# Keys of the second batch projected 64 tokens at a time, one halved step instead of two, and another order of work

## The chip, the cores and the metric

The kernel runs on one core of a Trainium2 chip. The time is that of the device, in microseconds (us), for one launch; the measure is the median of several executions. The core has five engines that run side by side, each taking its own instructions in the order in which they were written: TensorE (PE in the profile; its weight loads are listed apart as PEld), VectorE (DVE), ScalarE (ACT), GpSimd (POOL), and SyncE (SP), which here issues all transfers between memory and the chip. They wait for each other through semaphores.

## The reference

Linear attention over four batches of 1088 tokens, whose features are outer products of two small projections, followed by a gated two-layer network:

```python
def phi(x):
    a = np.einsum('rd,bhsd->bhsr', S1, x)
    b = np.einsum('rd,bhsd->bhsr', S2, x)
    return np.einsum('bhsi,bhsj->bhsij', a, b).reshape(*x.shape[:-1], r * r)
q_p, k_p = (phi(q), phi(k))                     # r = 8, 64 features
kv = np.einsum('bhsf,bhsd->bhfd', k_p, v)
z = np.sum(k_p, axis=2)
num = np.einsum('bhsf,bhfd->bhsd', q_p, kv)
den = np.einsum('bhsf,bhf->bhs', q_p, z)[..., None] + 1e-06
x = (num / den), reshaped to 4352 tokens x 128
h = x @ w_in                                    # 128 x 2048
g = h * np.clip(h + 3.0, 0.0, 6.0) / 6.0
out = g @ w_out                                 # 2048 x 128
```

## The kernel before

The whole schedule is written out by hand: `ORDER` is a string of some 1,070 names, and `Plan.run` emits one operation after the other in that order. As each engine takes its own instructions in program order, `ORDER` fixes for each engine what comes behind what. A name may carry a choice after a colon: `:V` puts the operation on VectorE instead of its first engine, `:a`, `:h`, `:o` choose the bank of PSUM. `warm` is a matmul of ones that nobody reads (L284).

The inputs arrive as loads (`ld_...`, L324), all issued by SyncE in the order of the string: keys k0 to k7 (two pieces for each batch), values v0 to v7, queries q0 to q8, and the weights in five blocks of w_in (wi0 to wi4) and four of w_out (wo0 to wo3). A load waits until its buffer is free: the weights' raw words have 4 buffers, the keys 3, the values 3. Weights come as 64-bit words that hold float32; `scale`, `rest` (ScalarE or VectorE), `shift` (VectorE), `word` (GpSimd or VectorE), `high` (ScalarE) and `low` (GpSimd or VectorE) turn a block into a high and a low part, since each large product is done as three matmuls: high x high, low x high, high x low.

For each batch the keys are projected (`mm_k`, L377), copied out (`cp_k`), their outer products made (`outer_k`), and summed against the values on TensorE, tile by tile of 128 tokens (`kvt_b_i`, L407 and L410); `twice_b`, `fold_b` and `keep_b` bring the sum into the form that the queries use. `mm_k` projects a tile of 128 tokens in pieces of KEY_COLS[b] tokens; s_all, 64 columns, is what streams. Batch 0 takes pieces of 64, batches 1 to 3 pieces of 32.

The 4352 tokens form nine chunks. Chunk 0 goes the near way (`tr`, `trcp`, `nd`, `norm`, `xt`), with `halves` (L438) bringing the first batch's sum to it; the others go the far way (`proj`, `cp`, `prod`, `invert`, `divide`, `outer`, `turn`, `move`, `xmm`), where `move` is a set of transfers within the chip. `xhi` and `xlo` split x into two parts. Then come eight steps for each chunk, two blocks of 128 hidden units each: `h` and `l` (L632, L633, L636) form h in a bank of type h, of which there are two; `relu` (ScalarE), `gate` (VectorE), `ghi` (ScalarE or VectorE) and `glo` (GpSimd or VectorE) form the gated value and its two parts; `o` and `p` (L669) add up the output, `out` brings it out of PSUM and `store` writes it. A step that is halved (chunk below HALVED, step below FIRST) makes its h in two halves of 256 tokens, so that it can begin when half of x is there; its parts are named `h_c_step_block_half`.

```python
halved = c < HALVED and fp < FIRST
for r, u in product(range(2 if halved else 1), range(2)):
    i, k = (r * n // 2, (r + 1) * n // 2) if halved else (0, n)
```

Of the kernel before, what the change touches and what calls it, by code (L numbers as in the profile page):

```python
# [107 lines left out]
fold_1 cp_k5 outer_k5_0:V h_0_1_1_0 turn_1_0 high_wi3 ghi_0_3 h_0_1_0_0 l_0_1_0_0 outer_1_1 h_0_1_0_1 turn_1_1 l_0_1_1_0 ld_q3 h_0_2_1 l_0_2_1
scale_wi4 outer_k5_4:V h_0_2_0 l_0_2_0 shift_wi4 keep_1 low_wi3 h_0_1_1_1 l_0_1_1_1 outer_k5_2:V relu_0_2 ld_q2 l_0_1_0_1 relu_0_1 o_0_3 gate_0_2
ld_wo0 rest_wo0 rest_wi4 scale_wo0 mm_k4 gate_0_1 move_1 proj_23:o:a cp_2_1 cp_2_0 shift_wo0 h_0_5_1 l_0_5_1 ld_k6 ld_v4 h_0_5_0 ghi_0_2 glo_0_2:V  # L110
cp_3_1 h_0_4_1 cp_3_0 glo_0_3 l_0_5_0 word_wi4 l_0_4_1 high_wi4 low_wi4 cp_k4 h_0_4_0 l_0_4_0 relu_0_5 gate_0_5 p_0_3 relu_0_4 gate_0_4 o_0_2 p_0_2
ghi_0_1 xmm_1:o:a xhi_1_0 xlo_1_0 xhi_1_1 xlo_1_1 word_wo0 h_0_6_1 l_0_6_1 high_wo0 h_0_6_0 l_0_6_0 outer_k4_0:V h_1_1_0 ghi_0_0 outer_k4_2:V ld_v5
ld_q4 l_1_1_0 h_1_1_1 relu_0_6 l_1_1_1 prod_3 invert_3 glo_0_1 relu_1_1 gate_0_6 kvt_2_0 kvt_2_1 kvt_2_2 kvt_2_3 kvt_2_4 kvt_2_5 kvt_2_6 mm_k6 cp_k6
kvt_2_7 low_wo0 kvt_2_8 twice_2 h_1_2_0 l_1_2_0 ghi_0_4 glo_0_0:V glo_0_4 gate_1_1 h_1_2_1 l_1_2_1 relu_1_2 p_0_1 ghi_1_1 prod_2 p_0_0 h_1_3_0
outer_k6_0:V l_1_3_0 h_1_3_1 ld_v6 ld_q7 l_1_3_1 relu_1_3 ld_k7 divide_3 outer_3_1 gate_1_2 outer_3_0 glo_1_1:V o_0_1 gate_1_3 ld_wo3 ld_v7 h_0_7_1
invert_2 ghi_1_2 h_0_7_0 l_0_7_0 ld_wo2 scale_wo2 l_0_7_1 relu_0_7 o_0_0 outer_k6_2:V h_1_0_1 h_1_0_0 l_1_0_0 gate_0_7 turn_3_1 rest_wo3 l_1_0_1
fold_2 out_0_3 mm_k7 kvt_3_0 kvt_3_1 h_1_7_1 glo_1_2 turn_3_0 divide_2 outer_2_0 outer_2_1 h_1_7_0 l_1_7_0 l_1_7_1 o_1_2 ghi_1_3 glo_1_3:V relu_1_0
p_1_2 gate_1_0 relu_1_7 p_1_3 h_1_5_0 l_1_5_0 ld_q5 gate_1_7 ghi_1_0 glo_1_0 turn_2_1 turn_2_0 cp_k7:V h_1_5_1 scale_wo3 outer_k7_2:V l_1_5_1 keep_2
o_1_1 shift_wo3 h_1_6_1 shift_wo2 word_wo3:V rest_wo2 l_1_6_1 h_1_6_0 l_1_6_0 word_wo2 p_1_1 o_1_0 ghi_0_7 outer_k7_4 p_1_0 relu_1_5 gate_1_5 o_1_3
h_1_4_0 l_1_4_0 ghi_0_5 outer_k7_0:V glo_0_7:V h_1_4_1 l_1_4_1 high_wo3:V high_wo2 out_1_3 move_3 low_wo2:V ghi_0_6 glo_0_6 proj_45:a:o cp_4_1  # L120
relu_1_6 cp_5_1 kvt_3_2 kvt_3_3 kvt_3_4 kvt_3_5 kvt_3_6 cp_4_0 kvt_3_7 kvt_3_8 twice_3 cp_5_0 gate_1_6 move_2 xmm_23:o:a xhi_3_1 fold_3 o_0_4 relu_1_4
xhi_3_0:V h_3_1_1 h_3_1_0 xlo_3_1 xlo_3_0 l_3_1_0 low_wo3 glo_0_5:V p_0_6 xhi_2_0 xlo_2_0 l_3_1_1 gate_1_4 xhi_2_1 ghi_1_6 relu_3_1 glo_1_6 gate_3_1
p_0_4 o_0_6 ghi_1_4 xlo_2_1 glo_1_4:V h_3_3_0 h_3_3_1 l_3_3_1 prod_4 l_3_3_0 relu_3_3 p_0_5 ld_q6 invert_4 divide_4 h_3_0_0 l_3_0_0 o_0_7 p_0_7
outer_4_0 gate_3_3 ghi_3_1 glo_3_1:V o_1_6 h_3_0_1 l_3_0_1 h_2_0_1 l_2_0_1 h_2_0_0 p_1_6 relu_3_0 l_2_0_0 relu_2_0 ghi_1_7:V keep_3 gate_3_0 o_0_5
ghi_1_5 h_2_1_0 l_2_1_0 glo_1_7 prod_5 gate_2_0 h_2_1_1 l_2_1_1 p_1_7 glo_1_5 out_0_7 h_3_2_0 l_3_2_0 h_3_2_1 l_3_2_1 p_1_4 relu_2_1 gate_2_1 relu_3_2
o_1_5 invert_5 ghi_3_3:V h_3_5_0 l_3_5_0 o_1_4 glo_3_3 h_3_5_1 gate_3_2 l_3_5_1 o_1_7 ghi_2_1 glo_2_1:V divide_5 relu_3_5 gate_3_5 h_2_3_0 l_2_3_0
h_2_3_1 l_2_3_1 relu_2_3 p_1_5 p_3_1 gate_2_3 o_3_1 outer_4_1 ghi_3_2 glo_3_2:V h_3_6_1 h_3_6_0 l_3_6_1 ghi_3_0 glo_3_0 l_3_6_0 relu_3_6 outer_5_1
# [638 lines left out]
```

## Time and profile before

| | us |
|---|---|
| median of 3 runs | 225.82 |
| lowest and highest | 225.63, 226.63 |
| the profiled execution, its own time | 226.31 |
| its span, first to last instruction | 224.4 |
| TensorE busy in the span | 218.4 (97%) |
| VectorE busy | 182.2 (81%) |
| ScalarE busy | 147.7 (66%) |
| GpSimd busy | 144.2 (64%) |

The span is the stretch between the first and the last instruction that the profiler saw; the time of the execution is 1.9 us longer. Durations below come from this one execution. A matmul's end is modelled, so the distance from one start to the next tells more than the duration of one.

### The profile page before, as it was taken

The page shows a single profiled execution, that of the slowest core. Times are in us where ns is not written, and L with a number is a line of the kernel's source. Part 1 is how long each engine was busy: PE and PEld are TensorE (multiplying, and loading weights), DVE is VectorE, ACT ScalarE, POOL GpSimd, SP SyncE. Part 2 cuts the span into 40 slices and gives each one's busy share as a digit, 9 for nine tenths or more (in the row PEclk, how much of TensorE's full clock was granted, in tenths as well). Part 3 has the DMA queues.
Part 4 walks back from the last instruction along what each step waited for, and adds up shares of the span by engine and source line. Part 5 has one row for each costly group of instructions (what it writes and reads, how often), then busy time and mean ns, then how long its engine had stood idle before and what let it go on. Part 6 is the DMA issues. An engine that isn't in the chain of part 4 may idle for free.

```text
span 224.4 us, 4722 instructions
## 1 busy us (share of the span) xinstructions
PE 218.4 (97%) x1885; PEld 175.5 (78%) x1885; DVE 182.2 (81%) x244; ACT 147.7 (66%) x201; POOL 144.2 (64%) x103
## 2 busy tenths in 40 slices
...
DMA packets 9429, 17.76 MB, mean 79 GB/s; under 512 B 1728, under 2 KB 2368, under 8 KB 9408
## 3 DMA queue, kind: packets, MB, share of 16 engines
...
## 4 chain that ended last, share of the span: by engine, by line
PE 93%; DMA 2%; SPq 1%; ACT 1%; issue 1%
PE o L669 42%; PE h L632 14%; PE h L633 14%; PE h L636 14%; DMA raw<-weights_dram 2%; PE o L407 2%; PE a L377 2%; PE a L546 1%; PE a L551 1%; SPq L324 1%; PE o L551 1%; ACT w L339 1%; PE o L546 0%; PE h L513 0%; PE o L501 0%
## 5 line engine op out<-in xcount | busy, mean ns | idle before, releaser
L652 POOL TENSOR_TENSOR gl<-g,gh 128x1024 fp32r<-128x1024 f32 (+1 forms) x39 | 92.1, 2364 | 60.9 <-ACT gh L254 34.2
L646 DVE SCALAR_TENSOR_TENSOR g<-g,h 128x1024 f32<-128x1024 f32 (+1 forms) x72 | 82.6, 1154 | 20.1 <-ACT g L643 19.7
L643 ACT ACTIVATE g<-h 128x1024 f32<-128x1024 f32 (+1 forms) x72 | 70.1, 979 | 36.6 <-PE h L636 23.9
L254 ACT CAST gh<-g 128x1024 fp32r<-128x1024 f32 (+1 forms) x53 | 53.2, 1011 | 19.3 <-PE o L669 16.7
L632 PE MATMUL h<-xh,wi_hi 128*128 128x512 f32 (+1 forms) x148 | 55.8, 378 | 0.0
L633 PE MATMUL h<-xh,wi_lo 128*128 128x512 f32 (+1 forms) x148 | 55.0, 373 | 0.0
L669 PE MATMUL o<-gh,wo_hi 128*128 128x512 f32 (+1 forms) x144 | 54.3, 381 | 0.0
L669 PE MATMUL o<-gh,wo_lo 128*128 128x512 f32 (+1 forms) x144 | 54.0, 378 | 0.0
L636 PE MATMUL h<-xh,wi_hi 128*128 128x512 f32 (+1 forms) x148 | 52.7, 372 | 0.0
L652 DVE TENSOR_TENSOR gl<-g,gh 128x1024 fp32r<-128x1024 f32 (+1 forms) x33 | 40.8, 1238 | 4.6 <-ACT gh L254 3.6
L669 PE MATMUL o<-gl,wo_hi 128*128 128x512 f32 (+1 forms) x144 | 40.9, 379 | 0.0
L632 PEld LDWEIGHTS h<-xh,wi_hi 128*128 128x128 f32 x148 | 27.8, 188 | 7.1 <-DVE g L646 0.6
L633 PEld LDWEIGHTS h<-xh,wi_lo 128*128 128x128 f32 x148 | 27.9, 188 | 4.7
L636 PEld LDWEIGHTS h<-xh,wi_hi 128*128 128x128 f32 x148 | 27.6, 188 | 5.0
L669 PEld LDWEIGHTS o<-gh,wo_hi 128*128 128x128 f32 x144 | 27.1, 188 | 5.5 <-issue 0.4
L669 PEld LDWEIGHTS o<-gh,wo_lo 128*128 128x128 f32 x144 | 27.1, 188 | 4.9
L669 PEld LDWEIGHTS o<-gl,wo_hi 128*128 128x128 f32 x144 | 25.9, 188 | 5.1 <-DVE gl L652 0.4
L254 DVE CAST gh<-g 128x1024 fp32r<-128x1024 f32 (+1 forms) x19 | 14.9, 785 | 3.5 <-PE o L669 3.3
L595 POOL TENSOR_TENSOR qph<-ab 128x512 f32<-128x512 f32 (+1 forms) x16 | 16.4, 1038 | 0.3
L354 POOL TENSOR_TENSOR w<-w,r 128x512 int32<-128x512 int32 (+1 forms) x8 | 9.8, 1230 | 3.9 <-DVE w L350 2.4
L387 DVE TENSOR_TENSOR kph<-a,ab 128x512 f32<-128x512 f32 (+1 forms) x15 | 9.3, 642 | 2.3 <-ACT ab L254 2.2
L602 DVE STREAM_TRANSPOSE raw<-qph 128x512 f32<-128x512 f32 (+1 forms) x16 | 10.2, 660 | 0.2
...
## 6 DMA issues: line engine op xcount, KB each, us to landing
raw<-weights_dram SPq DMA_DIRECT2D x7, 512.0 KB, 6.7
...
qT<-tokens_dram SPq DMA_DIRECT2D x8, 256.0 KB, 5.1
outT_dram<-os SPq DMA_DIRECT2D x8, 256.0 KB, 2.1
...
kT<-tokens_dram SPq DMA_DIRECT2D x4, 320.0 KB, 4.7
v<-tokens_dram SPq DMA_DIRECT2D x4, 264.0 KB, 4.7
kT<-tokens_dram SPq DMA_DIRECT2D x4, 256.0 KB, 4.8
```

Of the source, the lines that this page charges most:

```text
L254: (nc.scalar.copy if e == ACT else engines[e].tensor_copy)(out, src)
L354: engines[e].tensor_tensor(w, w, at(rb)[:, :n], op=ALU.add)
L387: engines[e].tensor_tensor(out, a_, b_, op=ALU.mult)
L595: engines[e].tensor_tensor(out, a_, b_, op=ALU.mult)
L602: nc.vector.transpose(turned_view()[:, :, r * half : (r + 1) * half].rearrange("p f (t w) -> p t f w", w=Q), src)
L632: nc.tensor.matmul(at(hb)[:, u, i:k], wi_hi[:, f], x, start=True, stop=False)
L633: nc.tensor.matmul(at(hb)[:, u, i:k], wi_lo[:, f], x, start=False, stop=False)
L636: nc.tensor.matmul(at(hb)[:, u, i:k], wi_hi[:, f], at(x_buf[c])[:, 1, i:k], start=False, stop=True)
L643: nc.scalar.activation(at(gb)[:, :, :n], at(hb)[:, :, :n], AF.Relu, bias=3.0, scale=1.0)
L646: nc.vector.scalar_tensor_tensor(at(gb)[:, :, :n], at(gb)[:, :, :n], 6.0, at(hb)[:, :, :n], op0=ALU.min, op1=ALU.mult)
L652: engines[e].tensor_tensor(at(gl)[:, :, :n], at(gb)[:, :, :n], at(gh)[:, :, :n].bitcast(F32), op=ALU.subtract)
L669: nc.tensor.matmul(at(ob)[:, :n], w, x[:, :n], start=left == acc["all"] and i == 0, stop=left == 1 and i == len(pairs) - 1)
```

## The change

Three things. FIRST goes from 2 to 1: only step 0 of chunk 0 is still halved, step 1 is made of whole matmuls of 512 tokens. KEY_COLS[1] goes from 32 to 64: the keys of the second batch (k2 and k3) are projected in half as many pieces, twice as wide. And the string `ORDER` is replaced from its first name to about the start of chunk 7; the last lines are the same but for some choices of VectorE or GpSimd. (The two kernels have the same number of operations otherwise: eight `warm`, and the same loads.) The diff, with the order cut to its first part:

```diff
 HALVED = 1
-FIRST = 2
+FIRST = 1
...
-KEY_COLS = (HP, Q, Q, Q)
+KEY_COLS = (HP, HP, Q, Q)
...
 ORDER = """
-s_copy warm warm warm warm warm warm s_rep ld_k0 ld_k1 warm mm_k0:a cp_k0 outer_k0_0 outer_k0_2:V mm_k1:a cp_k1 outer_k1_2 outer_k1_0:V ld_q0 mm_q0:h
-ld_v0 kvt_0_0 kvt_0_1 ld_wi1 kvt_0_2 cp_q0 outer_q0_0:V outer_k1_4 ld_v1 scale_wi1 shift_wi1 rest_wi1 s_tr s_back ld_wi0 scale_wi0 word_wi1 high_wi1
-warm kvt_0_3 kvt_0_4 kvt_0_5 kvt_0_6 outer_q0_2:V kvt_0_7 kvt_0_8 twice_0 rest_wi0:V tr_0_0:o trcp_0_0 shift_wi0 low_wi1:V tr_0_2:h spread word_wi0
-ld_wi2 rest_wi2:V scale_wi2 high_wi0 fold_0 zmm shift_wi2 word_wi2 ld_q1 halves nd_0_0:o trcp_0_2 nd_0_2:h low_wi0:V norm_0_0 keep_0 proj_1:a:o ld_wo1
-scale_wo1 shift_wo1 xt_0_0:h rest_wo1 norm_0_2 word_wo1 cp_1_0 xhi_0_0 high_wi2 ld_k2 ld_k3 mm_k2 cp_k2 cp_1_1 xt_0_2 xlo_0_0 mm_k3 h_0_0_1_0 high_wo1
-low_wi2 l_0_0_1_0 xhi_0_1:V xlo_0_1 h_0_0_1_1 h_0_0_0_0 cp_k3 ld_wi3 ld_v2 prod_1 outer_k3_2 low_wo1 l_0_0_0_0 outer_k2_2:V scale_wi3 h_0_0_0_1
-l_0_0_0_1 outer_k2_0:V l_0_0_1_1 relu_0_0 outer_k3_4:V ld_k4 ld_v3 outer_k3_0:V invert_1 divide_1 h_0_3_0 l_0_3_0 rest_wi3 h_0_3_1 l_0_3_1 relu_0_3
...
+s_rep ld_k0 warm warm warm warm mm_k0:a ld_k1 mm_k1:h cp_k0 outer_k0_0 ld_q0 mm_q0:h ld_v0 outer_k0_2:V cp_k1 outer_k1_0:V cp_q0 ld_wi1 ld_v1 kvt_0_0
+kvt_0_1 kvt_0_2 rest_wi1 ld_wi0 s_tr scale_wi1 s_back ld_wi2 outer_k1_2:V outer_k1_4 rest_wi0 kvt_0_3 kvt_0_4 kvt_0_5 kvt_0_6 kvt_0_7 kvt_0_8
+outer_q0_0:V tr_0_0:h shift_wi1 word_wi1:V spread warm scale_wi0 high_wi1 warm twice_0 fold_0 zmm s_copy shift_wi0 low_wi1:V trcp_0_0:V rest_wi2:V
+outer_q0_2 tr_0_2:a warm word_wi0 scale_wi2 high_wi0 halves nd_0_0:h trcp_0_2 nd_0_2:h shift_wi2 word_wi2 keep_0 ld_q1 proj_1:a:a warm low_wi0:V
+norm_0_0 xt_0_0:o ld_wo1 scale_wo1 shift_wo1 ld_wi3 rest_wo1 word_wo1 high_wi2 rest_wi3 ld_k2 norm_0_2 xt_0_2 xhi_0_0 cp_1_1 mm_k2 cp_1_0 prod_1
+high_wo1 low_wi2:V cp_k2 ld_k3 mm_k3 xlo_0_0 xhi_0_1 h_0_0_1_0 l_0_0_1_0 h_0_0_0_0 l_0_0_0_0 invert_1 ld_wi4 h_0_0_0_1 cp_k3 xlo_0_1 outer_k2_0:V
+low_wo1 divide_1 l_0_0_0_1 scale_wi4 h_0_3_1 outer_k2_2:V h_0_0_1_1 l_0_0_1_1 h_0_3_0 outer_k3_0:V rest_wi4 l_0_3_1 outer_k3_2:V outer_k3_4 l_0_3_0
+outer_1_1 scale_wi3 shift_wi3 word_wi3 relu_0_0 ld_v2 ld_v3 ld_k5 shift_wi4 kvt_1_0:a kvt_1_1 kvt_1_2 kvt_1_3 kvt_1_4 kvt_1_5 kvt_1_6 kvt_1_7 kvt_1_8
...
```

Taken from the whole string, SyncE's loads and moves stand in this order up to the second far group:

```
before: k0 k1 q0 v0 wi1 v1 wi0 wi2 q1 wo1 k2 k3 wi3 v2 k4 v3 k5 wi4 q3 q2 wo0 move_1 k6 v4 v5 q4 v6 q7 k7 wo3 v7 wo2 q5 move_3
after:  k0 k1 q0 v0 wi1 v1 wi0 wi2 q1 wo1 wi3 k2 k3 wi4 v2 v3 k5 wo0 q3 q2 wo3 k4 move_1 v6 v4 v5 k7 k6 q5 wo2 v7 q4 move_3
```

ScalarE's first operations:

```
before: cp_q0 scale_wi1 rest_wi1 s_back scale_wi0 high_wi1 twice_0 trcp_0_0 scale_wi2 high_wi0 halves trcp_0_2 keep_0 scale_wo1 rest_wo1 xhi_0_0
        high_wi2 cp_k2 high_wo1 cp_k3 scale_wi3 relu_0_0 rest_wi3 relu_0_3 twice_1
after:  cp_q0 rest_wi1 scale_wi1 s_back rest_wi0 scale_wi0 high_wi1 twice_0 scale_wi2 high_wi0 halves trcp_0_2 keep_0 scale_wo1 rest_wo1 high_wi2 rest_wi3
        xhi_0_0 high_wo1 cp_k2 xhi_0_1 cp_k3 scale_wi4 rest_wi4 scale_wi3 relu_0_0 relu_0_3 twice_1
```

And TensorE's, from the summing of the first batch to that of the third:

```
before: warm kvt_0_3 .. kvt_0_8 tr_0_0 tr_0_2 fold_0 zmm nd_0_0 nd_0_2 proj_1 xt_0_0 mm_k2 xt_0_2 mm_k3, steps 0_0 and 0_3, kvt_1 mm_k5 fold_1,
        steps 0_1 and 0_2, o_0_3 mm_k4 proj_23, ..., xmm_1, ..., kvt_2_0 .. kvt_2_6 mm_k6 kvt_2_7 kvt_2_8, ..., fold_2 mm_k7 kvt_3_0 kvt_3_1
after:  kvt_0_3 .. kvt_0_8 tr_0_0 warm warm fold_0 zmm tr_0_2 warm nd_0_0 nd_0_2 proj_1 warm xt_0_0 xt_0_2 mm_k2 mm_k3, steps 0_0 and 0_3, kvt_1 mm_k5 fold_1,
        steps 0_2 and 0_1, proj_23 o_0_3, ..., mm_k4 xmm_1, ..., kvt_2_0 .. kvt_2_8 mm_k6 mm_k7, ..., fold_2
```

## Rows read from the trace of the kernel before

**Rows 1.** Windows: us; busy PE, PEld, DVE, ACT, POOL; granted clock, DMA share, GB/s.

```profile
0.00:14.71 14.71, 11.93 (x221) 7.87 (x222) 7.97 (x22) 8.46 (x23) 8.30 (x20) 1.00 0.86 317
14.71:221.20 206.49, 206.47 (x1664) 167.67 (x1663) 174.27 (x224) 138.88 (x177) 135.87 (x84) 1.00 0.20 63
221.20:224.40 3.20, 0.00 (x0) 0.00 (x0) 0.00 (x0) 0.38 (x1) 0.00 (x0) 0.81 0.12 41
```

**Rows 2.** Waits of TensorE before 14.8: waiting line, releaser, us, times, longest.

```profile
PE o L501 <- ACT kvb L438: 0.6, 1, 0.6
PE h L513 <- issue: 0.5, 1, 0.5
```

**Rows 3.** The chain that ended last, 14.2 to 16.6: start, us, what.

```profile
14.21 0.50 issue
...
14.98 0.58 PE a L377 x32
15.56 0.37 PE h L513 x2
15.93 0.70 PE a L377 x40
```

**Rows 4.** Timeline of ScalarE, 8 to 13: start, us, what, tiles.

```profile
8.12 0.42 ACT L344 ACTIVATE r<-raw 128x256 int32<-128x256 uint32 x1
...
9.32 0.44 ACT L339 ACTIVATE w<-raw 128x256 f32<-128x256 f32 x1 [0.62 <-DMA raw<-weights_dram]
...
9.96 0.26 ACT L441 COPY kvt<-o 128x128 f32<-128x128 f32 x1
...
11.58 0.43 ACT L438 COPY kvb<-a 64x66 f32<-64x66 f32 x2
```

**Rows 5.** Timeline of TensorE: warm matmuls, projections, h in halves and whole.

```profile
0.77 1.44 PE L284 MATMUL o<-const-bfloat16-1.0 128*128 128x512 bf16 x3 [0.77 <-PEq L755]
...
5.90 0.69 PE L377 MATMUL h<-s_all,qT 128*64 128x64 f32 x16 [0.20 <-DMA qT<-tokens_dram]
...
14.91 0.65 PE L377 MATMUL a<-s_all,kT 128*32 128x64 f32 x32
...
16.78 0.28 PE L633 MATMUL h<-xh,wi_lo 128*128 128x256 f32 x1
...
17.61 0.28 PE L632 MATMUL h<-xh,wi_hi 128*128 128x256 f32 x1
...
18.32 0.40 PE L633 MATMUL h<-xh,wi_lo 128*128 128x512 f32 x1
...
19.25 0.39 PE L636 MATMUL h<-xh,wi_hi 128*128 128x512 f32 x1
```

**Rows 6.** SyncE's issues (start, us): k2 with k3; wi3; k6; v6.

```profile
6.40 1.08 SPq L324 DMA_DIRECT2D kT<-tokens_dram  x2
8.57 0.33 SPq L324 DMA_DIRECT2D raw<-weights_dram  x1
...
30.41 0.53 SPq L324 DMA_DIRECT2D kT<-tokens_dram  x1
...
32.49 0.38 SPq L324 DMA_DIRECT2D v<-tokens_dram  x1
```

**Rows 7.** DMA issues: KB each, us from issue to landing: k3, wi3, k6, v6.

```profile
kT<-tokens_dram SPq DMA_DIRECT2D x1, 320.0 KB, 7.7
raw<-weights_dram SPq DMA_DIRECT2D x1, 512.0 KB, 7.4
kT<-tokens_dram SPq DMA_DIRECT2D x1, 256.0 KB, 3.0
v<-tokens_dram SPq DMA_DIRECT2D x1, 264.0 KB, 5.4
```

**Rows 8.** Timeline of TensorE in the third batch's sums.

```profile
36.34 0.22 PE L410 MATMUL o<-ab 128*32 128x32 f32 x2
36.56 0.32 PE L407 MATMUL o<-kph,v 128*32 128x64 f32 x8
```

More of the change, by code (lines that the diff above doesn't have):

```diff
@@ L108 @@
[L108 to L127, printed above, removed]
@@ new lines @@
+high_wo1 low_wi2:V cp_k2 ld_k3 mm_k3 xlo_0_0 xhi_0_1 h_0_0_1_0 l_0_0_1_0 h_0_0_0_0 l_0_0_0_0 invert_1 ld_wi4 h_0_0_0_1 cp_k3 xlo_0_1 outer_k2_0:V
+low_wo1 divide_1 l_0_0_0_1 scale_wi4 h_0_3_1 outer_k2_2:V h_0_0_1_1 l_0_0_1_1 h_0_3_0 outer_k3_0:V rest_wi4 l_0_3_1 outer_k3_2:V outer_k3_4 l_0_3_0
+outer_1_1 scale_wi3 shift_wi3 word_wi3 relu_0_0 ld_v2 ld_v3 ld_k5 shift_wi4 kvt_1_0:a kvt_1_1 kvt_1_2 kvt_1_3 kvt_1_4 kvt_1_5 kvt_1_6 kvt_1_7 kvt_1_8
+relu_0_3 gate_0_0 gate_0_3 turn_1_1 mm_k5 twice_1 cp_k5 fold_1 high_wi3 ld_wo0 rest_wo0 h_0_2_1 l_0_2_1 h_0_2_0 keep_1 l_0_2_0 ld_q3 h_0_1_1 l_0_1_1
@@ new lines @@
+outer_1_0 turn_1_0 ld_q2 ld_wo3 low_wi3 h_0_1_0 l_0_1_0 ld_k4 proj_23:o:a ghi_0_3 glo_0_3 word_wi4:V o_0_3 relu_0_2 high_wi4 gate_0_2 cp_3_0 relu_0_1
+gate_0_1 h_0_4_0 l_0_4_0 cp_3_1 ghi_0_2 glo_0_2:V cp_2_0 h_0_4_1 l_0_4_1 p_0_3 move_1 h_0_5_1 ld_v6 l_0_5_1 ghi_0_0 cp_2_1 relu_0_4 h_0_5_0 l_0_5_0
+scale_wo0 o_0_2 outer_k5_4 outer_k5_0 relu_0_5 shift_wo0 gate_0_4 p_0_2 outer_k5_2 mm_k4 ghi_0_1 xmm_1:o:a low_wi4 h_0_6_1 xhi_1_0 l_0_6_1 gate_0_5
+ld_v4 xhi_1_1 h_0_6_0 xlo_1_0 l_0_6_0 ld_v5 h_1_1_1 xlo_1_1 h_1_1_0 l_1_1_1 l_1_1_0 ld_k7 cp_k4 outer_k4_0:V kvt_2_0 outer_k4_2:V kvt_2_1 kvt_2_2
@@ new lines @@
+kvt_2_3 kvt_2_4 kvt_2_5 kvt_2_6 kvt_2_7 ld_k6 prod_3 invert_3 glo_0_1 ld_q5 kvt_2_8 relu_0_6 gate_0_6 glo_0_0:V relu_1_1 mm_k6 mm_k7 word_wo0 high_wo0
+scale_wo3 low_wo0:V ghi_0_4 h_1_2_0 l_1_2_0 prod_2 ld_wo2 divide_3 h_1_2_1 rest_wo2 l_1_2_1 gate_1_1 o_0_1 cp_k6 outer_k6_0:V relu_1_2 gate_1_2
+glo_0_4 p_0_1 ghi_1_1 glo_1_1:V h_1_3_0 h_1_3_1 l_1_3_1 twice_2 l_1_3_0 relu_1_3 p_0_0 h_0_7_1 ghi_1_2 ld_v7 o_0_0 outer_3_1 out_0_3 outer_3_0
+gate_1_3 h_0_7_0 invert_2 l_0_7_1 ld_q4 l_0_7_0 turn_3_1 h_1_0_0 l_1_0_0 outer_k6_2:V relu_0_7 h_1_0_1 glo_1_2 l_1_0_1 o_1_2 p_1_1 rest_wo3 divide_2
@@ new lines @@
+gate_0_7 outer_2_0 relu_1_0 outer_2_1 turn_3_0 move_3 p_1_2 h_1_7_1 l_1_7_1 ghi_1_3 fold_2 o_1_3 h_1_7_0 l_1_7_0 cp_k7 gate_1_0 ghi_1_0 h_1_5_0
+h_1_5_1 glo_1_3:V outer_k7_4 p_1_3 turn_2_0 l_1_5_1 l_1_5_0 o_1_0 turn_2_1 relu_1_7 move_2 gate_1_7 h_1_6_0 scale_wo2 shift_wo3 shift_wo2 glo_1_0
+outer_k7_2:V h_1_6_1 relu_1_5 l_1_6_1 gate_1_5 ghi_0_7 outer_k7_0:V o_1_1 p_1_0 out_1_3 l_1_6_0 h_1_4_1 l_1_4_1 glo_0_7:V word_wo2 keep_2 high_wo2:V
+h_1_4_0 l_1_4_0 proj_45:o:a cp_5_0 cp_4_0 word_wo3 cp_5_1 cp_4_1 ghi_1_5 relu_1_6 gate_1_6 kvt_3_0 ghi_0_5 kvt_3_1 kvt_3_2 kvt_3_3 kvt_3_4 high_wo3
@@ new lines @@
+kvt_3_5 kvt_3_6 kvt_3_7 kvt_3_8 twice_3 xmm_23:o:a xhi_3_1 xhi_3_0 fold_3 low_wo2 xhi_2_0 xlo_2_0 xlo_3_1 keep_3 glo_0_5 o_0_4 o_0_5 xlo_3_0 h_3_1_1
+ghi_0_6 l_3_1_1 xhi_2_1:V p_0_5 relu_1_4 gate_1_4 low_wo3 o_0_7 ghi_1_6 h_3_1_0 l_3_1_0 ghi_1_4 h_3_3_0 h_3_3_1 l_3_3_1 glo_0_6:V p_0_7 l_3_3_0 prod_4
+invert_4 p_0_4 p_0_6 glo_1_6:V relu_3_1 gate_3_1 o_1_5 xlo_2_1 o_1_6 relu_3_3 gate_3_3 ghi_3_3 h_3_0_1 l_3_0_1 glo_1_5 h_3_0_0 l_3_0_0 relu_3_0
+h_2_0_1 glo_1_4:V p_1_5 gate_3_0 ghi_3_1 o_0_6 out_0_7 l_2_0_1 ghi_3_0 glo_3_1:V h_2_0_0 l_2_0_0 divide_4 p_1_4 prod_5 h_2_1_0 h_2_1_1 relu_2_0
@@ new lines @@
+ghi_3_6:V l_2_7_1 l_2_7_0 relu_2_7 gate_2_7 o_3_2 glo_3_6 out_3_3 h_2_2_1 l_2_2_1 h_2_2_0 l_2_2_0 o_3_6 p_2_1 h_3_7_1 l_3_7_1 relu_2_2 gate_2_2
+ghi_2_2 glo_2_2 glo_2_3:V invert_6 h_3_7_0 move_4 l_3_7_0 relu_3_7 gate_3_7 h_3_4_1 h_3_4_0 divide_6 ghi_2_0 l_3_4_1 p_2_3 move_5 l_3_4_0 o_2_3
+xmm_45:a:a relu_3_4 prod_7 xhi_5_1 xlo_5_1 o_2_2 xhi_4_1:V h_2_6_0 h_2_6_1 xhi_5_0:V p_3_5 l_2_6_0 xhi_4_0:V xlo_4_0 ghi_2_7 l_2_6_1 relu_2_6 o_2_0
+gate_3_4 xlo_4_1 ghi_3_7 outer_6_1 invert_7 glo_2_0 o_2_1 gate_2_6 h_2_5_1 ghi_2_6 h_2_5_0 l_2_5_0 glo_3_7:V p_2_0 p_3_6 xlo_5_0 l_2_5_1 relu_2_5
@@ new lines @@
+gate_2_5 glo_2_7 h_4_0_0 l_4_0_0 h_4_0_1 l_4_0_1 relu_4_0 gate_4_0 p_3_7 p_2_2 o_3_7 h_4_1_1 h_4_1_0 l_4_1_0 l_4_1_1 out_2_3 divide_7 h_4_3_1 l_4_3_1
+outer_7_1 ghi_3_4 glo_3_4:V h_4_3_0 l_4_3_0 relu_4_1 ghi_4_0 o_3_4 glo_4_0 p_2_7 o_2_7 gate_4_1 relu_4_3 gate_4_3 p_3_4 out_3_7 ghi_4_1 h_4_2_1
+l_4_2_1 h_4_7_0 glo_4_1:V l_4_7_0 h_4_2_0 l_4_2_0 relu_4_2 turn_7_1 gate_4_2 o_4_0 h_4_7_1 l_4_7_1 relu_4_7 o_2_6 gate_4_7 ghi_4_7:V outer_7_0 ghi_2_5
+turn_7_0 outer_6_0 turn_6_0 p_4_0 proj_8:a:a cp_8_0 o_4_1 h_4_5_1 l_4_5_1 h_4_5_0 l_4_5_0 turn_6_1 glo_2_6 h_5_1_0 relu_4_5 gate_4_5 l_5_1_0 h_5_1_1
```

59 lines of the change are left out of this document (26 added, 33 removed).

## The prediction

> **What bounds the kernel now.** I read the windows first, cut where the work changes character. From 14.71 to 221.20 TensorE is busy for 206.47 of 206.49 us, at the full granted clock [rows 1]. Nothing that any other engine or load does in that stretch holds TensorE up by more than hundredths, so an order cannot win time there: it can only keep that stretch as full as it is or make a hole. What an order can win lies before 14.71, where TensorE is busy for 11.93 us, and in the 3.20 us behind its last matmul [rows 1]. The tail (last output, last store) is the same in both strings but for choices of engine, and I take it as unchanged. So the question is when TensorE begins its unbroken run, whether that run stays unbroken, and whether it gets shorter.
>
> The list of TensorE's waits, cut before 14.8, and the chain show what starts the run. TensorE waits 0.6 us for ScalarE's copy of the first batch's sums (`halves`, L438), and 0.5 us with nothing that the profile can name, between the two transposes of `xt_0_0` [rows 2, 3]. The chain calls this "issue": no engine and no load releases it. A late packet of TensorE's own instructions would look like that. Behind it stand `mm_k2` (0.58), `xt_0_2` (0.37) and `mm_k3` (0.70), all needed work, and then the first h at about 16.6 [rows 3].
>
> **The wider key pieces.** `mm_k2` and `mm_k3` go from 32 tokens a piece to 64, which takes away half of 72 matmuls and half of their weight loads. The nearest rows are two projections of four tiles each: `mm_q0`, already 64 wide, takes 0.69 us for 16 matmuls, `mm_k2`, 32 wide, 0.65 us for 32 [rows 5]. The same four tiles cost the same: four narrow pieces lie side by side in the array in the time of two wide ones. So the gain is 0; bounds from these rows are -0.1 to +0.1 for the 9 tiles. It only shortens the instruction stream.
>
> **The second step no longer halved.** Twelve matmuls of 256 columns become six of 512. Seven starts of 256 columns lie between 16.78 and 17.61, 0.119 apart; four of 512 between 18.32 and 19.25, 0.233 apart [rows 5]. That is 1.42 us against 1.40: a gain of 0.02 on the path. The halves' cover (beginning on half of x) is not needed for step 1, since it now comes after step 2, some 6 us later than x.
>
> **The start: the first batch's sums.** In the order before, ScalarE waits for wi0 until 9.32, does `scale_wi0`, `high_wi1`, and begins `twice_0` at 9.96; `halves` follows at 11.58 [rows 4]. In the new order `rest_wi0`, which VectorE did, stands on ScalarE between that landing and `scale_wi0`. The same operation on wi1 starts at 8.12 and is listed with 0.42; operations on ScalarE overlap by about 0.1, so it pushes `twice_0` back by 0.3. `trcp_0_0` leaves ScalarE for VectorE, but it stood behind `twice_0`, and `halves` waits for `fold_0` and `zmm`, which wait for `twice_0`. So I have `halves` at 11.9 instead of 11.58, and `nd`, `norm` and `xt` 0.3 later. The "issue" wait sits at the same instruction of TensorE's stream (the eight `warm` all stand ahead of `xt_0_0` in both strings, so the number of instructions up to it is the same) and ends at about 14.7 whatever comes before, so for `xt_0_0` it covers the delay. `xt_0_2` does feel it: x's second half comes at about 15.1. From there `xt_0_2` (0.37), `mm_k2` and `mm_k3` (0.58 + 0.70, less one switch between transposes and projections of about 0.1, since they now stand together) [rows 3] give the first h at 16.7 to 16.8, against 16.6: **+0.2**, bounds -0.4 (if the "issue" wait goes and `halves` doesn't move) and +0.5.
>
> **The start: loads.** wi3 now goes ahead of k2 and k3. It still waits for wi1's buffer and is issued at 8.57 at the earliest, and SyncE's queue holds k2 and k3 behind it, which were issued from 6.40 [rows 6]. This costs no bandwidth, since k3 landed at 6.95 + 7.7 = 14.6 and wi3 at 8.57 + 7.4 = 16.0 [rows 6, 7]: the queue is full to the end. But the three pieces are the same in both orders, so the last of them lands at about 16.0, and now that is k3. `mm_k3` is wanted at 15.1 + 0.37 + 0.5 = 16.0. It is an even race; a loss of 0 to 0.5, of which I put nothing into the sum, since the +0.2 is what covers it. On ScalarE `rest_wi3` now stands ahead of `xhi_0_0`, and wi3 as first of the three lands at about 14.4: `xhi_0_0` follows at about 15.1, in time. Then `scale_wi4`, `rest_wi4` and `scale_wi3` stand ahead of `relu_0_0`. wi4 is next, 512 KB at the pace between k3 and wi3 (1.4 us for 512 KB [rows 7]): 17.4. Three operations of 0.6 give `relu_0_0` at 19.2, the gate at 20.2 to 21.3, and the bank of h is wanted at about 22. In time, by 0.7 us.
>
> **Later: the third batch's loads.** Before, the burst behind `move_1` begins with k6 at 30.41, landing at 33.4; its fifth load, v6, lands at 32.49 + 5.4 = 37.9, that is 7.5 us after the burst's first issue [rows 6, 7]. Now k6 is the fifth (v6, v4, v5, k7, k6; 60 KB more), so it lands some 7.7 us after the first issue. The turns ahead of `move_1` no longer stand behind an outer product on VectorE, so I let the burst begin 0.4 earlier, at 30.0: k6 at 37.7. `mm_k6` now follows all nine tiles of `kvt_2`, at about 37.1 to 37.3. That is a hole of 0 to 1.0 us; I take **0.2**, nearer the small end, since the pace of the burst hangs on when the moves end. Against it stands the gap of 0.2 us in `kvt_2` between 36.34 and 36.56 [rows 8], which is not the pitch of its neighbours and looks like a wait for v5; v5 stays third of its burst, with the burst earlier: **-0.1**. Putting `mm_k7` and the two first tiles of `kvt_3` next to their likes takes away a switch or two of about 0.1 each, but `proj_23` and `mm_k4` part, and I take 0.
>
> **The rest.** Everything else moves work between ScalarE, VectorE and GpSimd, or along TensorE's queue. The cover of all that is the full run of rows 1: as long as no operand is late it costs nothing and gains nothing.
>
> **Sum.** +0.2 (first h) - 0.02 (halves) + 0.2 (k6) - 0.1 (v5) = +0.3 on the profiled execution's 226.31, so 226.6; that one lies 0.5 above the median of 225.82, so as a median 226.1.
>
> **Rivals.** (1) *The start gets earlier.* If the "issue" wait (0.5, with the time around it up to 0.7) moves off the path and `halves` isn't delayed, the first h comes at about 16.0. For it: such a wait depends on when a packet arrives. Against it: the same number of instructions stands ahead of it. It gives 225.82 - 0.6 = 225.2. More than that the order can't win, since TensorE's run holds the same matmuls. (2) *ScalarE's queue waits for loads, and TensorE with it.* The place is `scale_wi4` and `rest_wi4` ahead of `relu_0_0`, `relu_0_3` and `twice_1`. It decides if wi4 lands later than about 17.9: the gate then frees the bank of h too late. One load more ahead of it, 1.4 us [rows 7], makes it 18.8, and about 0.9 of that reaches TensorE; with k6 late by the full 1.0 and nothing made up, since TensorE has no idle time left to make it up with, the time is 225.82 + 0.2 + 0.9 + 0.4 to 1.0 = 227.3 to 227.9. For it: loads that nothing waited for now stand ahead of the path's own work. Against it: my landing times leave 0.5 us. (3) *TensorE's clock rises later.* Three warm matmuls of 512 columns take 1.44 us at the start, 0.48 each, against 0.233 for 512 columns later [rows 5]: they run at the 1.2 GHz level and the later ones at 2.4. Seven of them stood in a row; now there are four, and TensorE then idles until the first keys, with the others spread over the gaps behind `tr_0_0`. If the clock rises only after the first batch's sums, the transposes, `zmm` and `nd` on the path, some 1.5 us, take twice as long: up to +1.5, of which loads hide part, and I take 1.0: 227.1. If it rises before 9.3, when wi0 lands, it costs nothing, because that landing is what the start waits for [rows 4]. The Trainium skill (TensorE: Matmul & The Clock Gate, "What's actually happening") says that the throttled state is the default and activity releases it, and so speaks against taking warm matmuls away; no run here shows how many are enough. (4) *The new order does nothing where it was meant to*, with TensorE's run intact and all terms cancelling: 225.8, inside the forecast's range.
>
> **Chances.** Forecast, with (4) as its near end (225.6 to 226.7): 0.62. (1): 0.14. (2): 0.17. (3): 0.07. The range reaches from (1) to the near end of (2): 225.1 to 227.3. About 0.5%, 1.1 us, is what a measurement of this kernel can tell from no change: below 224.7 is faster, above 226.95 slower. (1) lies within it; only an earlier start and a shorter run together would go below, 0.04. Slower: most of (2), half of (3) and the far end of the forecast, 0.2. Same: 0.76.
>
> **What would show each step.** The windows of the new kernel: TensorE's run should begin at 14.7 to 15.1 and be full; a hole of over 0.3 us near 22 is rival (2), one near 37 the k6 term. `twice_0` should start at about 10.3 and `halves` at 11.9; `mm_k2` should take what it took, in half the instructions. The first pitch of 0.23 us for 512 columns, or of the key projections' pairs, tells when the clock rose. The prediction is wrong if TensorE's run has holes in chunks 2 to 8, where I have no term at all, or if the first h comes before 16.

## The result and the profile after

The median goes from 226.02 us (9 runs, 225.47 to 226.63) to **227.28 us** (9 runs, 226.57 to 227.88): a ratio of 1.0054, with an interval of 1.0037 to 1.0072. The new order is 1.26 us slower. The profiled execution took 227.37 us, its span is 225.6, against 226.31 and 224.4 before.

The windows of the new kernel, cut where those of [rows 1] are cut (its last matmul starts 1.2 later):

```profile
0.00:14.71 14.71, 12.35 (x222) 8.78 (x222) 8.10 (x22) 9.14 (x25) 7.54 (x19) 1.00 0.88 321
14.71:222.40 207.69, 206.42 (x1621) 167.30 (x1621) 171.19 (x219) 138.28 (x178) 141.38 (x87) 1.00 0.20 62
222.40:225.60 3.20, 0.00 (x0) 0.00 (x0) 0.00 (x0) 0.38 (x1) 0.00 (x0) 1.00 0.12 41
```

The tail is the same 3.20. TensorE is busy for longer ahead of 14.71 (12.35 against 11.93, for 222 matmuls against 221, of which the early ones run slower, as rival 3 has it), and its run behind it is 1.20 longer with the same busy time: 207.69 less 206.42 is 1.27 of idle time, where [rows 1] has 0.02. The list of TensorE's waits (line, releaser, us, times, longest) names most of it:

```profile
PE a L376 <- DMA kT<-tokens_dram: 1.4, 1, 1.4
PE a L409 <- issue: 1.0, 1, 1.0
PE o L283 <- PEq L754: 0.8, 1, 0.8
PE o L512 <- DVE x L508: 0.4, 1, 0.4
```

The first and third stand at the very start, ahead of the first keys. The 1.0 at L409 is new, and "issue" again is what no engine and no load explains. TensorE's timeline (start, us, what; the releaser in brackets) places it:

```profile
14.10 0.38 PE L512 MATMUL o<-ident,x 128*128 128x128 f32 x2
14.87 0.44 PE L512 MATMUL o<-ident,x 128*128 128x128 f32 x2 [0.39 <-DVE x L508]
15.32 1.57 PE L376 MATMUL a<-s_all,kT 128*64 128x64 f32 x36
16.83 0.39 PE L631 MATMUL h<-xh,wi_hi 128*128 128x256 f32 x1
...
20.76 0.19 PE L409 MATMUL a<-ab 128*32 128x32 f32 x1
21.92 0.22 PE L409 MATMUL a<-ab 128*32 128x32 f32 x1 [0.97 <-issue]
21.92 0.36 PE L406 MATMUL a<-kph,v 128*32 128x64 f32 x10
```

In the middle of `kvt_1`, between two matmuls of one line with the same operands, 1.16 lie from one start (20.76) to the next (21.92). What came meanwhile is seen among the DMA queues (packets, MB, share of the 16 engines). The whole kernel's q8 lines, before and after:

```profile
q8 instruction: 15, 0.25, 0.4%
```

```profile
q8 instruction: 14, 0.23, 0.4%
```

A packet of q8 is 16 KB. The windows count 3770 matmuls and weight loads before and 3686 after, some 250 to 260 for each packet. TensorE's wait in [rows 3] stands behind 443 of them, the one here behind 695, which is 252 more. So I read the packets of q8 as TensorE's instructions, a block of some 250 in each. The queues of the new kernel between 14.0 and 19.5, and between 19.5 and 20.6:

```profile
q1 hardware_dynamic: 875, 2.27, 103.3%
...
q1 hardware_dynamic: 191, 0.41, 103.1%
q8 instruction: 1, 0.02, 5.3%
```

The second packet is moved from 19.57 to 20.50, and TensorE goes on 1.4 later. In the kernel before the same second packet is moved from 16.30 to 17.24, 3.3 earlier; its queues between 16.2 and 17.3:

```profile
q1 hardware_dynamic: 101, 0.22, 74.9%
q8 instruction: 1, 0.02, 5.3%
```

The wait of [rows 3] at 14.21 is the same thing one packet earlier: moved 12.33 to 13.26, TensorE on at 14.71. In the new kernel that first packet comes at 11.44 to 12.31, and the 0.5 is gone.

**The sum.** The first h comes at 16.83 against 16.56 (+0.27). From there to the last matmul's start it is 205.26 against 204.34: the hole adds 1.16 (one pitch, that is from one start to the next, nearly all idle), the rest of the run is 0.25 shorter, the gap of [rows 8] being gone. 0.27 + 1.16 - 0.25 = 1.18, and the spans differ by 1.2.

### The profile page after: what moved, and what is told of

Its sections match the earlier page's. It is cut to its first block, busy times and chain, and to the rows that moved or that the text cites. A ratio compares the mean times of both kernels' runs of the same rounds, so it can differ in the third digit from the quotient of the medians.

```text
span 225.6 us, 4646 instructions
## 1 busy us (share of the span) xinstructions
PE 218.8 (97%) x1843; PEld 176.1 (78%) x1843; DVE 179.3 (79%) x240; ACT 147.8 (66%) x203; POOL 148.9 (66%) x105
## 4 chain that ended last, share of the span: by engine, by line
PE 95%; DVE 1%; DMA 1%; issue 1%; ACT 0%; SPq 0%
PE o L668 42%; PE h L631 14%; PE h L632 14%; PE h L635 14%; PE o L406 2%; PE a L376 2%; PE a L550 1%; DMA kT<-tokens_dram 1%; PE h L376 1%; PE o L545 1%; PE a L545 1%; PE o L550 1%; PE a L406 1%; DVE x L508 0%; PE a L444 0%
## 5 line engine op out<-in xcount | busy, mean ns | idle before, releaser
L651 POOL TENSOR_TENSOR gl<-g,gh 128x1024 fp32r<-128x1024 f32 (+1 forms) x40 | 96.7, 2422 | 58.1 <-PE o L668 22.8
L253 ACT CAST gh<-g 128x1024 fp32r<-128x1024 f32 (+1 forms) x54 | 54.2, 1010 | 13.9 <-DVE g L645 10.0
L631 PE MATMUL h<-xh,wi_hi 128*128 128x512 f32 (+1 forms) x146 | 55.1, 378 | 0.0
L635 PE MATMUL h<-xh,wi_hi 128*128 128x512 f32 (+1 forms) x146 | 51.7, 375 | 0.0
L651 DVE TENSOR_TENSOR gl<-g,gh 128x1024 fp32r<-128x1024 f32 (+1 forms) x32 | 40.2, 1256 | 1.8 <-ACT gh L253 1.5
L631 PEld LDWEIGHTS h<-xh,wi_hi 128*128 128x128 f32 x146 | 27.4, 188 | 6.6 <-issue 0.4
L635 PEld LDWEIGHTS h<-xh,wi_hi 128*128 128x128 f32 x146 | 27.3, 188 | 5.1
L632 PEld LDWEIGHTS h<-xh,wi_lo 128*128 128x128 f32 x146 | 27.4, 188 | 4.8
L594 POOL TENSOR_TENSOR qph<-ab 128x512 f32<-128x512 f32 (+1 forms) x16 | 19.0, 1200 | 0.3
L253 DVE CAST gh<-g 128x1024 fp32r<-128x1024 f32 (+1 forms) x18 | 13.9, 777 | 0.5
L353 POOL TENSOR_TENSOR w<-w,r 128x512 int32<-128x512 int32 (+1 forms) x7 | 8.8, 1262 | 4.5 <-DVE w L349 3.6
L386 DVE TENSOR_TENSOR kph<-a,ab 128x512 f32<-128x512 f32 x11 | 7.2, 681 | 2.5 <-ACT ab L253 2.5
```

Of the source, the lines that this page charges most:

```text
L253: (nc.scalar.copy if e == ACT else engines[e].tensor_copy)(out, src)
L353: engines[e].tensor_tensor(w, w, at(rb)[:, :n], op=ALU.add)
L386: engines[e].tensor_tensor(out, a_, b_, op=ALU.mult)
L594: engines[e].tensor_tensor(out, a_, b_, op=ALU.mult)
L631: nc.tensor.matmul(at(hb)[:, u, i:k], wi_hi[:, f], x, start=True, stop=False)
L632: nc.tensor.matmul(at(hb)[:, u, i:k], wi_lo[:, f], x, start=False, stop=False)
```

## Experiments

**The theory.** What differs is when loads are issued. SyncE's queue (start, us) in the kernel before, and then in the new one:

```profile
9.47 0.39 SPq L324 DMA_DIRECT2D kT<-tokens_dram  x1
10.59 0.33 SPq L324 DMA_DIRECT2D v<-tokens_dram  x1
15.62 0.33 SPq L324 DMA_DIRECT2D kT<-tokens_dram  x1
16.06 0.37 SPq L324 DMA_DIRECT2D raw<-weights_dram  x1
```

```profile
8.77 0.92 SPq L323 DMA_DIRECT2D kT<-tokens_dram  x2
9.91 0.33 SPq L323 DMA_DIRECT2D raw<-weights_dram  x1
10.28 0.91 SPq L323 DMA_DIRECT2D v<-tokens_dram  x2
11.23 0.58 SPq L323 DMA_DIRECT2D kT<-tokens_dram  x1
14.03 0.33 SPq L323 DMA_DIRECT2D raw<-weights_dram  x1
14.59 0.94 SPq L323 DMA_DIRECT2D qT<-tokens_dram  x2
```

Before, k4 (9.47) takes the last free key buffer, and k5 waits in SyncE's queue until `mm_k2` frees one: from 10.92 to 15.62 nothing is issued, and the packet comes soon after the loads have thinned out. In the new order k4 stands last of the group, so k5 goes out at 11.23, wo0 at 14.03, q3 and q2 from 14.59. The theory (P in the expectations): the packet waits behind the loads that are out by then, arrives 3.3 late, and TensorE runs out of instructions. Rivals: something else in the new order of work (O), the start (S, with the late clock C and the race for k3), the width of the pieces (W). Below, an edit shows steps of ORDER, one to a line; medians and ratios are against the kernel before on the same chip.

**The load order alone, taken back in the new kernel.**

```diff
 ld_v3
+ld_k4
 ld_k5
...
 l_0_1_0
-ld_k4
 proj_23:o:a
```

> The changed kernel with one load moved: k4 stands ahead of k5, so that k5, and wo0, q3 and q2 behind it, wait until mm_k2 has freed a key buffer at about 15.8 instead of being issued from 11.2 to 15. Theory P (TensorE's packet of instructions is asked for at about 14.1 and queues behind every load issued by then): fewer loads stand ahead of it, it is served at about 17.7 instead of 19.6 and can be used by 20; the wait of 1.0 us in kvt_1 goes, the time falls by about 1.1 to 226.1. Rival O (the wait belongs to the new order of work or to the number of instructions, not to the loads): it stays, 227.3. Rival S (the time is lost at the start, by the first h): the first h doesn't move, 227.3.

Measured: 226.90 against 226.20, 1.0037 (1.0014 to 1.0060). Its SyncE queue stands still in one row from 11.34, while k4 and k5 share it:

```profile
11.34 5.17 SPq L323 DMA_DIRECT2D kT<-tokens_dram  x2
```

The packet is moved at 18.07 to 19.64, and TensorE's timeline has no stop in `kvt_1`. The run from the first h to the last matmul falls from 205.26 to 204.73. But the first h is at 16.97, and TensorE waits for k6 ahead of `mm_k6`:

```profile
37.52 0.22 PE L406 MATMUL o<-kph,v 128*32 128x64 f32 x1
37.85 0.37 PE L376 MATMUL a<-s_all,kT 128*32 128x64 f32 x11
```

The hole goes, as the theory has it, but the time falls by about 0.4 (0.0017 of 226), a third of the 1.1 expected, and the two intervals overlap. A new wait has come in the hole's place. TensorE would begin `mm_k6` at about 37.5, 0.9 earlier than in the new kernel (38.39), and k6 lands at 37.80 and not at 36.91: the burst behind the moves begins at 29.79 here and at 28.92 there.

**That wait taken away too.** As above, and k6 issued first of its burst:

```diff
 move_1
+ld_k6
 h_0_5_1
...
 kvt_2_7
-ld_k6
 prod_3
```

> The first held kernel (k4 ahead of k5) with one more load moved: k6 first behind move_1 instead of fifth. In the first held kernel mm_k6 waited 0.33 us for k6 at 37.5. Theory P with the prediction's term for k6: that wait goes, all else stays, 0.3 less than the first held kernel, so 0.3% to 0.4% over the kernel before becomes 0.1% to 0.25%. Rival (the wait was for something else, or moves to v4 and v5): no change.

Measured: 226.38 against 226.31, 1.0003 (0.9981 to 1.0025). The window that held the hole is full, and the run is short of it:

```profile
14.71:221.60 206.89, 206.33 (x1624) 167.24 (x1621) 171.28 (x220) 138.62 (x180) 141.67 (x87) 1.00 0.20 63
20.76:21.92 1.16, 1.16 (x93) 1.07 (x82) 1.16 (x3) 0.75 (x3) 1.16 (x1) 1.00 0.98 358
```

Two loads put elsewhere undo the loss, with the first h still late (17.02) and the run down to 204.15; the interval lies below that of the new kernel (1.0037 to 1.0072). Everything else in the change, taken together, costs nothing that can be measured.

**The load order alone, put into the kernel before.** No step of an engine moves, only two loads:

```diff
 outer_k3_4:V
-ld_k4
+ld_k5
 ld_v3
...
 kvt_1_1
-ld_k5
 gate_0_0
...
 ld_wo0
+ld_k4
 rest_wo0
```

> The kernel before, all work in its old order, with two loads changed: k5 stands where k4 stood, and k4 behind wo0, so that SyncE isn't held by a key buffer and issues wi4, q3, q2 and wo0 by about 14 instead of from 15.6. Theory P: TensorE's packet now queues behind them, comes at about 19.5 instead of 16.3 and is usable at about 21.5 to 22, while TensorE needs it at 20.0: a wait of 1.5 to 2 us in or behind kvt_1, time 227.4 to 228.0. Rival O: nothing of the order of work is changed, so 226.0 within 0.3. Rival S: the first h is where it was, 226.0.

Measured: 227.32 against 226.20, 1.0046 (1.0005 to 1.0088), with single runs from 226.04 to 229.47. The packet that was moved at 16.30 is now moved from 18.42 to 19.37, and `kvt_1` has its hole, as TensorE's timeline shows:

```profile
19.84 0.24 PE L407 MATMUL o<-kph,v 128*32 128x64 f32 x2
20.60 0.38 PE L407 MATMUL o<-kph,v 128*32 128x64 f32 x8 [0.52 <-issue]
```

So the loads make the hole without the rest of the change. Set beside the kernel before, start for start, TensorE falls back by 0.73 here, and behind the first h by 0.2 or more nowhere else. The hole is half as wide as the 1.5 to 2 that I expected, since the packet came at 18.42 and not at 19.5. The median moved by 1.1, but its interval begins close to 1, and the traced execution, 226.69, is one of the faster ones; what the slower ones lost was not traced.

**The width, taken back in the new kernel.**

```diff
-KEY_COLS = (HP, HP, Q, Q)
+KEY_COLS = (HP, Q, Q, Q)
```

> The changed kernel with the key pieces of the second batch back at 32 tokens, all else as changed: 72 TensorE instructions more between the place where the packet is asked for and the place where it is needed. Theory P: the packet comes at the same time (19.6, usable at 21.9), TensorE runs dry 72 instructions, about 0.4 us, earlier: the wait grows to 1.4 to 1.6 us, time 227.7. Rival W (the wider pieces themselves cost the time): the wait goes or the projections get shorter, 226.0 to 226.5. Rival S: 227.3.

Measured: 230.27 against 226.20, 1.0202 (1.0134 to 1.0271, from four runs). I expected 227.7, with one longer wait in `kvt_1`; it came otherwise. Not through the projections: 72 narrow matmuls from 15.75 to the first h at 16.89 take 1.14, where 36 wide ones that need not wait for k3 take 1.20 (in the last attempt below, 15.36 to 16.56). The wait in `kvt_1` is 0.7 and not 1.4 to 1.6, for the packet came at 19.08. But with 72 more instructions (matmuls and weight loads) the packets' boundaries fall elsewhere, and TensorE meets a second late packet, as the list of waits shows:

```profile
PE a L376 <- issue: 1.1, 1, 1.1
...
PE a L406 <- issue: 0.7, 1, 0.7
```

The larger one ends at 40.34, behind a packet moved from 38.16 to 39.10. This packet was not held up for long: by the count of instructions TensorE entered the block ahead of it at about 37.3, but it ran through that block, mostly narrow projections, by 39.02. In this order the wider pieces are worth about 1.5% then (1.0202 against 1.0054). The trace shows no faster matmuls in that, only a shorter stream whose boundaries fall better. But it is of the fastest of the four executions, 229.01, which is 1.6 above that of the new kernel; what the slower ones lost is open.

**The width alone, in the kernel before** (`KEY_COLS = (HP, HP, Q, Q)`, nothing else).

> The kernel before with the key pieces of the second batch at 64 tokens, nothing else. Theory P: the projections take as long as they did (0.58 and 0.70 us with what follows), 72 instructions fewer only make the boundary come later where there was no wait: 226.0, within 0.2 of the kernel before. Rival W (wider pieces are slower or faster by themselves): off by 0.3 or more.

Measured: 226.07 against 226.31, 0.9992 (0.9963 to 1.0020): nothing. Its profiled execution, 227.52, happened to be one with a late start. The first loads landed late (ScalarE begins on wi0 at 10.30, 9.32 in [rows 4]), and so did the first packet (13.83 to 14.79, 1.5 later than in the profile of before): "issue" at `xt_0_0` is 0.98, and the first h comes at 18.11, 1.55 later. About 1.0 of that stands ahead of `xt_0_0` already, 0.5 is the longer wait for the packet. The run from there is 204.12.

**Pieces of 128** (`KEY_COLS = (HP, P, Q, Q)` in the new kernel).

> The changed kernel with the second batch's keys projected 128 tokens at a time: 36 TensorE instructions fewer than in the changed kernel between the place where the packet is asked for and the place where it is needed. Theory P: the packet comes at the same time, TensorE reaches the boundary 36 instructions, some 0.2 us, later: the wait shrinks from about 1.1 to 0.9, time 227.1. Rival W (the width of the pieces itself matters): off by more than 0.4 either way.

Measured: 228.31 against 226.51, 1.0070 (1.0035 to 1.0105), over a microsecond above the expected 227.1. The stream is shorter still, but these pieces are slower, and rival W holds here: 18 of them take 2.03 to the first h, in TensorE's timeline:

```profile
15.80 2.22 PE L376 MATMUL a<-s_all,kT 128*128 128x64 f32 x18
17.83 0.36 PE L631 MATMUL h<-xh,wi_hi 128*128 128x256 f32 x1
```

The packet's wait in `kvt_1` shrinks to 0.22, since TensorE gets there a microsecond later; 0.71 is lost to a move at 103.8, which I did not follow up.

**The clock** (rival 3): three of the later warm matmuls moved to the start of the new kernel.

```diff
 ld_k0
+warm
+warm
+warm
 warm
```

> The changed kernel with three of the later warm matmuls moved to the start, so that seven stand in a row there as before, and TensorE's clock should rise at about 4.7 instead of 8.7. Theory P: the start waits for wi0 at 9.1 either way, and the wait in kvt_1 stays: 227.3. Rival C (the late rise of the clock costs the time): 226.0 to 226.5.

Measured: 227.55 against 226.31, 1.0053 (1.0028 to 1.0079): as slow as the new kernel. The clock does rise earlier. `mm_q0` in TensorE's timeline of the new kernel, and then of this one:

```profile
6.17 1.07 PE L376 MATMUL h<-s_all,qT 128*64 128x64 f32 x16
```

```profile
5.66 0.69 PE L376 MATMUL h<-s_all,qT 128*64 128x64 f32 x16
```

And from its list of waits:

```profile
PE a L409 <- issue: 1.1, 1, 1.1
```

0.69 is what [rows 5] has. But the first h is at 16.91, and the wait in `kvt_1` is there, as expected: the packet comes at 19.69 to 20.62.

**The k3 race**: wi3 behind k3 again (`rest_wi3` with it).

```diff
-ld_wi3
...
 ld_k3
+ld_wi3
 mm_k3
```

> The changed kernel with k2 and k3 ahead of wi3 again, and rest_wi3 behind cp_k3 on ScalarE, so that the first h doesn't wait for k3. The first h should come at about 16.5 instead of 16.8. Theory P: the packet still comes at 19.6 and is usable at 21.9, so what the start wins is lost in kvt_1: the wait grows by 0.3, time 227.2 to 227.3. Rival S (the start carries through): 227.0 or less.

Measured: 226.86 against 226.20, 1.0032 (1.0008 to 1.0056). I missed on the first h: it is at 17.20, not earlier. With k2 and k3 issued from 6.05 the loads of the start land later: TensorE waits 0.64 and 0.25 for values, and ScalarE begins on wi0 at 9.91 (9.10 in the new kernel), so that `proj_1` starts at 14.07 instead of 13.28. These 0.8 are the loss; the first packet, late too (12.88 to 13.77), adds 0.18 of "issue" at `xt_0_0`, and half of it all is made up because `mm_k3` finds k3 there. The second packet is moved at 19.29 to 20.23, and as TensorE gets to it 0.4 later, it loses less there (TensorE's timeline):

```profile
21.14 0.19 PE L409 MATMUL a<-ab 128*32 128x32 f32 x1
21.50 0.22 PE L409 MATMUL a<-ab 128*32 128x32 f32 x1 [0.16 <-issue]
```

**The loads as in the kernel before, in the new order** (k2, k3, wi3, v2, k4, v3, then k5, wi4, wo0; the unpacking of wi3 and wi4 moved behind).

> The changed kernel with the loads issued in the order of the kernel before as far as its buffers allow (k2 k3 wi3 v2 k4 v3, then held by mm_k2: k5 wi4 wo0 q3 q2 wo3), rest_wi3 behind cp_k3 and the unpacking of wi4 behind high_wi3. Theory P: the packet asked for at 14.1 to 14.9 finds as few loads ahead of it as in the kernel before, comes by 17.5, and nothing waits in kvt_1; the first h no longer waits for k3: 226.0, like the kernel before. Rival O (the order of the work itself costs about 1 us): 227.0 or more. Rival S: the first h at 16.5 instead of 16.8 gives 227.0.

Measured: 227.34 against 226.31, 1.0052 (1.0024 to 1.0080), where I expected 226.0. The packet is early (16.41 to 17.64) and no packet is waited for, the first h is at 16.68; most of the gain is eaten by my own edit. ScalarE's timeline, and the new line in the list of waits:

```profile
22.57 0.68 ACT L338 ACTIVATE w<-raw 128x512 f32<-128x512 f32 x1
23.15 1.23 ACT L343 ACTIVATE r<-raw 128x512 int32<-128x512 uint32 x2
...
25.42 1.05 ACT L642 ACTIVATE g<-h 128x1024 f32<-128x1024 f32 x1
```

```profile
PE h L631 <- DVE g L645: 0.6, 1, 0.6
```

wi4's unpacking, moved later on ScalarE, holds `relu_0_2` until 25.42, its gate comes late, and the next h waits for its bank (a pitch of 0.99 at 26.79). That is the mechanism of rival 2, at another place than I gave it.

**An attempt at the best of both**: those loads, k6 first of its burst, wo3 behind k7, and the unpacking of wi4 and wo0 behind relus.

> The changed kernel with its loads in the order k2 k3 wi3 v2 k4 v3, held there by mm_k2, then k5 wi4 wo0 q3 q2; k6 first behind move_1 and wo3 behind k7; rest_wi3 behind cp_k3; the unpacking of wi4 behind relu_0_1, so that it doesn't stand ahead of relu_0_2 as it did in the kernel with the loads of before. Theory P: no wait for a packet in kvt_1, none of the gate at 26.8, none for k6; first h at 16.6 to 16.8, TensorE's run 204.2 long: 225.9 to 226.1, ratio 0.998 to 1.000 to the kernel before. Rival O (something else in the new order costs): 227.

Measured: 227.18 against 226.51, 1.0027 (1.0007 to 1.0047). Again a miss. No packet is waited for in `kvt_1` and the first h is at 16.56, but two new holes stand in the run: 0.50 at 24.54, where `proj_23` waits for q2 and q3, now issued later, and 0.65 at 33.17 for a gate. No version here is measurably faster than the kernel before.

**The new kernel once more**, beside those two.

> The changed kernel itself once more, beside the others, for a second trace of it. Theory P: a wait with no releaser of 0.7 to 1.2 us in or near kvt_1, ending 1.2 to 1.5 us after the packet that was fetched at about 19.5; time 227.3. Rival O: the wait was an accident of one execution and the time is lost elsewhere.

Measured: 227.65 against 226.51, 1.0044 (1.0021 to 1.0067), its packet at 19.64 to 20.57, its wait 1.10 ending at 22.08, as expected.

## Why the prediction was right and where it was wrong

The median lies at the upper end of the range, 1.2 above the forecast, and the change is slower by just over the 0.5% that I set: the side that I gave 0.20. The amount is rival 2's; the mechanism is none of mine. That the median lies inside the range, by 0.02, is luck: the terms that I added up came to 0.3, and the change cost 1.26.

**The step that failed** is "The rest": "as long as no operand is late it costs nothing". The stall is of instructions, not of operands. I had named the cause myself (the "issue" wait looks like a late packet of TensorE's instructions), but priced it at one place only and took it as fixed "whatever comes before". I did not ask where the next packet is needed, nor what the new load order does to its arrival. That was a term of 1.16, four times the sum I had. The Trainium skill (Runtime: NRT & Kernel Launch, "Instruction fetch mechanics") says that instructions come in blocks of 16 KB, 256 of them, and that crossing into the next block is mostly hidden. The size agrees with the packets of q8 here; the hiding fails in the stretch where loads fill the DMA engines (103% in the queue's row above): 0.5 before, 0.97 to 1.10 after.

**The "issue" wait at `xt_0_0`** was to stay; it went, since the first packet came 0.9 earlier. That is the condition of rival (1), and it brought nothing: `xt_0_2` waits 0.39 for x, and `mm_k3` for k3. What stood behind the wait was as late as the wait.

**The first h**: +0.27 measured, +0.2 forecast, for another reason. ScalarE in the new kernel, against [rows 4]:

```profile
9.10 0.46 ACT L343 ACTIVATE r<-raw 128x256 int32<-128x256 uint32 x1 [0.19 <-DMA raw<-weights_dram]
9.47 0.42 ACT L338 ACTIVATE w<-raw 128x256 f32<-128x256 f32 x1
...
10.10 0.27 ACT L440 COPY kvt<-o 128x128 f32<-128x128 f32 x1
...
11.57 0.43 ACT L437 COPY kvb<-a 64x66 f32<-64x66 f32 x2
...
19.00 1.96 ACT L642 ACTIVATE g<-h 128x1024 f32<-128x1024 f32 x2
```

`twice_0` is later by 0.14, not 0.3 (wi0 landed earlier), and `halves` stands at 11.57, where it stood: that delay never reached it. The 0.27 is the race that I left out of the sum. k3 lands at 15.96 (forecast 16.0), `mm_k3` was wanted at 15.79 (forecast 16.0) and starts at 16.10, a gap that the 36 starts of the 15.32 row show and the list of waits does not. (k3's issue in the kernel before, which I took as 6.95, is at 7.10, and its landing at 14.76; nothing hangs on that.)

**The key pieces**: 0, as forecast, by the run with the width alone. **Halves**: 0.02, too small to see.

**Rival 2's place**: wi4 lands at 17.2 (17.4), `relu_0_0` starts at 19.00 (19.2). In time, as forecast; nothing waits. The sign that I named for this rival, a hole of over 0.3 near 22, came all the same, from another cause, so it could not tell the two apart. **Rival 3**: the clock does rise later. The four warm matmuls take 1.86, 0.46 each (the 1.2 GHz level, by 0.233 for as many columns in [rows 5]; it is read from the pitches, since the windows' granted clock is 1.00 here too), and `mm_q0` 1.07 against 0.69; the pitches are full speed only from 8.7. That is just ahead of wi0's landing at 9.1, so it costs nothing, as I wrote for that case, and the run with seven in a row bears it out.

**k6**: not in the new kernel. The burst begins at 28.92 (forecast 30.0), k6 lands at 36.91 (37.7), and `mm_k6` starts at 38.39; even a microsecond earlier, without the hole, it would have found k6 there. The wait that I described came in the run with k5 held, where the burst begins at 29.79, k6 lands at 37.80, and TensorE loses 0.33 (forecast 0.2). **v5**: gone, as forecast; the run without its hole is 0.25 shorter, a bit more than the 0.1.
